# An H3 convolution with a gated linear unit, forward and backward, on one core: the GLU's forward pass moved four tiles ahead into the FFT stage, transposing loads for the weight gradients, one SBUF arena

## The chip, the core and the metric

The kernel runs on one core of a Trainium2 chip. The metric is the device time of one execution in microseconds. Names of engines: PE (TensorE, matrix products and transposes), DVE (VectorE), ACT (ScalarE), POOL (GpSimd), SP (SyncE, used here only to issue DMAs). SBUF is the on-chip memory of 128 partitions, PSUM the accumulators that PE writes and that DVE or ACT must copy out ("evacuate"); DRAM is off the core and reached by DMA alone.

## The reference, cut to what matters

Inputs are bf16; S = 2048 tokens, D = 512 channels, F = 1376 hidden units. The kernel returns the output and the gradients of nine inputs for a given `grad_out`.

```python
xn = layernorm(A_q)                                   # [S, D], no affine part
ks = sum_t shift(A_k, by 3-t tokens) * shift_k[:, t]  # 4 taps per channel
kv = ks * A_v
y  = irfft(rfft(pad(kv, 2S)) * rfft(pad(ssm_k, 2S)))[:S] + kv * ssm_D   # per channel
s  = xn * y
h  = sigmoid(xn @ w_gate) * (xn @ w_up)               # [S, F]
z  = h @ w_down                                       # [S, D]
out = A_q + s * silu(z)
# and the vjp of out with respect to q, k, v, shift_k, ssm_k, ssm_D, w_gate, w_up, w_down
```

The outputs are `out_0` (out), `out_1` to `out_3` (dq, dk, dv), `out_4` to `out_6` (the small gradients of shift_k, ssm_k, ssm_D), `out_7`, `out_8` (of w_gate, w_up, [512, 1376]) and `out_9` (of w_down, [1376, 512]).

## The kernel before, in words

**Tiles.** The 2048 tokens are 16 tiles of 128: partition p and tile j hold token 16p + j. The 512 channels are four groups `cg` of 128. F is padded to 1408, eleven blocks `fb` of 128. The FFT of length 4096 is done as matrix products with cosine and sine tables: `Cf` (forward, made at the start from integer tables, line 61), `Ci` (its transpose, for the inverse), and two small matrices `BD` and `R`.

**Stage 1, FFT forward and convolution.** For each channel group: the filter's block is transposed to token order (`KC`); step 1 multiplies by `Cf` (`ps_q`, L144, copied to `QgK` or `QgV`); PE transposes flip the axes (`ps_fl`, L156); step 3 multiplies by `BD` (`ps_xre`, `ps_xim`, copied to `KFg` or `Xc`). The shift convolution of k runs on DVE (`ks_term`, L352). DVE multiplies the two spectra (`cm_t`, L202 and 203, then `Y`, L208), PE goes back with `R` (`ps_b`, L179, 180) and `Ci` (`ps_y`, L193, 194). y goes to DRAM (`y_d`). Spectra go to DRAM too (`KF_d`, `KVF_d`), since the backward pass reads them. The order of these pieces is a list written by hand; transposes of the three GLU weights (L290, L295) are woven between them.

**Stage 2, the GLU, forward and backward, tile by tile.** LayerNorm (L438 to 447), `xnT` (L450), then `psG`, `psU` (L469, L473: the two projections), `sigT` (L476), `hT` (L477, h with F on the partitions), `psZ` (L507), the elementwise chain of the gate, `dz` and its transpose, `psD` (L562: dz by w_down), `dh` (L565), `dg` and `du` (L566, 567), `psX` (L579: back to dxn), the LayerNorm's gradient (`dxn` L583 to `goj` L594). For the weight gradients h, dg and du are also wanted with tokens on the partitions: `to_token_major` makes 33 PE transposes a tile (`ps_tmA`, `ps_tmB`, L489 and L493), copies them out (`stS_h`, `stS_dg`, `stS_du`) and stores them (`hS_d`, `dgS_d`, `duS_d`).

**Stages 3 and 4 together.** Two generators, interleaved one step to two: the FFT of the output's gradient and the inverse transforms for dkv and d ssm_k (same names, `B1g`, `B2g`; then `dksg`, the shift's gradient `dk_term` L755, the diagonal products), and the weight gradients: `psW` (L792) accumulates over the 16 token tiles from `L` (loads L786 of the token-major copies, 512 KB each) and `rhsA` (loads L780 of dz and of xn). The gradients of w_gate and w_up come out transposed there, with F on the partitions; 88 PE transposes (`ps_wT`, L803) and two copies (`w_ot`, `dwt`) turn them round.

PSUM is copied out by a fixed pattern of engines per call site (ACT alone, DVE alone, or two to one). SBUF is split in pools opened and closed by stage, so stage 2 starts when the pools of stage 1 are given back, and stage 3 after those of stage 2. The framework's scheduler puts each engine's instructions into one order; an engine works its own list in order.

Of the kernel before, what the change touches and what calls it, by code (L numbers as in the profile page):

```python
# [16 lines left out]
P = 128  # L17
# [12 lines left out]
JQ = 512 // GW  # L30
JC = 1
TC = JC * P
FPG = 512 // TC
# [8 lines left out]
def gen_fft_consts(nc, pre, fpool, tpool, pspool, ident):  # L42
    negpi = pre["negpi"]
    nc.vector.memset(negpi[:], -math.pi)
    sc = 2 * math.pi / 8192
    out = {}
    a = tpool.tile([P, 16], i32, name="cg_a")
    nc.gpsimd.iota(a[:], pattern=[[1, 16]], base=0, channel_multiplier=16)
    b = tpool.tile([P, 128], i32, name="cg_b")
    nc.gpsimd.iota(b[:], pattern=[[2, 128]], base=1, channel_multiplier=0)  # L50
    m = tpool.tile([P, 16, 128], i32, name="cg_m")
    nc.vector.tensor_tensor(m[:], a[:, :, None].to_broadcast([P, 16, 128]),
                            b[:, None, :].to_broadcast([P, 16, 128]), ALU.mult)
    mc = tpool.tile([P, 2, 16, 128], i32, name="cg_mc")
    nc.vector.tensor_single_scalar(mc[:, 0], m[:], 6144, ALU.add)
    nc.vector.tensor_single_scalar(mc[:, 0], mc[:, 0], 8191, ALU.bitwise_and)
    nc.vector.tensor_single_scalar(mc[:, 1], m[:], 8191, ALU.bitwise_and)
    mf = tpool.tile([P, 2, 16, 128], f32, name="cg_mf")
    nc.vector.tensor_copy(mf[:], mc[:])
    Cf = fpool.tile([P, 2, 16, 128], bf16, name="Cf")  # L60
    nc.scalar.activation(Cf[:], mf[:], ACT.Sin, bias=negpi[:], scale=sc)
    out["Cf"] = Cf
    Ci = fpool.tile([P, 2, 16, 128], bf16, name="Ci")
    out["Ci"] = Ci
    pi_ = tpool.tile([P, 1], i32, name="cg_pi")
    nc.gpsimd.iota(pi_[:], pattern=[[0, 1]], base=0, channel_multiplier=1)
    pa = tpool.tile([P, 1], i32, name="cg_pa")
    nc.vector.tensor_single_scalar(pa[:], pi_[:], 3, ALU.arith_shift_right)
    pe = tpool.tile([P, 1], i32, name="cg_pe")
    nc.vector.tensor_single_scalar(pe[:], pi_[:], 7, ALU.bitwise_and)  # L70
    paf = tpool.tile([P, 1], f32, name="cg_paf")
    nc.vector.tensor_copy(paf[:], pa[:])
    pef = tpool.tile([P, 1], f32, name="cg_pef")
    nc.vector.tensor_copy(pef[:], pe[:])
    cb = tpool.tile([P, 16, 8], f32, name="cg_cb")
    nc.gpsimd.iota(cb[:], pattern=[[1, 16], [0, 8]], base=0, channel_multiplier=0,
                   allow_small_or_imprecise_dtypes=True)
    ce = tpool.tile([P, 16, 8], f32, name="cg_ce")
    nc.gpsimd.iota(ce[:], pattern=[[0, 16], [1, 8]], base=0, channel_multiplier=0,
                   allow_small_or_imprecise_dtypes=True)  # L80
    ab = tpool.tile([P, 16, 8], i32, name="cg_ab")
    nc.vector.tensor_scalar(ab[:], cb[:], paf[:, 0:1], None, ALU.mult)
    mask = tpool.tile([P, 16, 8], f32, name="cg_mask")
    nc.vector.tensor_scalar(mask[:], ce[:], pef[:, 0:1], None, ALU.is_equal)
    ang = tpool.tile([P, 3, 16, 8], i32, name="cg_ang")
    nc.vector.tensor_single_scalar(ang[:, 0], ab[:], 12, ALU.add)
    nc.vector.tensor_single_scalar(ang[:, 1], ab[:], 8, ALU.add)
    nc.vector.tensor_copy(ang[:, 2], ab[:])
    nc.vector.tensor_single_scalar(ang[:], ang[:], 15, ALU.bitwise_and)
    angf = tpool.tile([P, 3, 16, 8], f32, name="cg_angf")  # L90
    nc.vector.tensor_copy(angf[:], ang[:])
    tri = tpool.tile([P, 3, 16, 8], f32, name="cg_tri")
    nc.scalar.activation(tri[:], angf[:], ACT.Sin, bias=negpi[:], scale=2 * math.pi / 16)
    nc.vector.tensor_tensor(tri[:], tri[:], mask[:, None, :, :].to_broadcast([P, 3, 16, 8]), ALU.mult)
    BD = pre["BD"]
    nc.vector.tensor_copy(BD[:], tri[:].rearrange("p t b e -> p t (b e)"))
    out["BD"] = BD
    R = pre["R"]
    trif = tri[:].rearrange("p t b e -> p t (b e)")
    nc.vector.tensor_scalar(R[:, 0, 0, :], trif[:, 0, :], SCALE_INV, None, ALU.mult)  # L100
    nc.vector.tensor_scalar(R[:, 0, 1, :], trif[:, 1, :], SCALE_INV, None, ALU.mult)
    nc.vector.tensor_scalar(R[:, 1, 0, :], trif[:, 2, :], SCALE_INV, None, ALU.mult)
    nc.vector.tensor_scalar(R[:, 1, 1, :], trif[:, 0, :], SCALE_INV, None, ALU.mult)
    out["R"] = R
    return out


class Evac:

    def __init__(self, nc, pattern="av"):  # L110
        self.nc = nc
        self.pattern = pattern
        self.i = 0

    def __call__(self, dst, src, eng=None):
        if eng is None:
            eng = self.pattern[self.i % len(self.pattern)]
            self.i += 1
        if eng == "a":
            self.nc.scalar.copy(dst, src)  # L120
        elif eng == "v":
            self.nc.vector.tensor_copy(dst, src)  # L122
        else:
            self.nc.gpsimd.tensor_copy(dst, src)


def gen_ci(nc, consts, pspool, ident):
    Cf, Ci = consts["Cf"], consts["Ci"]
    for c in range(2):
        for jh in range(2):  # L130
            pt = pspool.tile([P, 8, 128], bf16, name="ps_ci", tag="tr")
            for jj in range(8):
                nc.tensor.transpose(pt[:, jj, :], Cf[:, c, 8 * jh + jj, :], ident[:])
            nc.scalar.copy(Ci[:, c, 8 * jh:8 * jh + 8, :], pt[:])


def fft_fwd_step1_group(nc, consts, xsrc, cg, Qg, psum_pool, ev):
    Cf = consts["Cf"]
    for c in range(2):
        for jb in range(NJ // JQ):  # L140
            ps = psum_pool.tile([P, JQ, GW], f32, name="ps_q", tag="mm")
            for jj in range(JQ):
                j = jb * JQ + jj
                nc.tensor.matmul(ps[:, jj, :], Cf[:, c, j, :], xsrc(j), start=True, stop=True)  # L144
            src = ps[:].rearrange("p j (g e) -> p j g e", e=8)
            dst = Qg[:, c, :, jb * JQ:(jb + 1) * JQ, :].rearrange("p g j e -> p j g e")
            ev(dst, src)


def fft_flip_group(nc, Qg, Qf, ident, psum_pool, ev):  # L150
    for c in range(2):
        for gb in range(GG // 8):
            pt = psum_pool.tile([P, 8, 128], bf16, name="ps_fl", tag="tr")
            for gi in range(8):
                g = gb * 8 + gi
                nc.tensor.transpose(pt[:, gi, :], Qg[:, c, g].rearrange("p j e -> p (j e)"), ident[:])  # L156
            ev(Qf[:, c, gb * 8:(gb + 1) * 8, :], pt[:])


def fft_fwd_step3_chunk(nc, consts, Qf, qq, psum_pool):  # L160
    BD = consts["BD"]
    qre = Qf[:, 0, 4 * qq:4 * qq + 4, :].rearrange("p g k -> p (g k)")
    qim = Qf[:, 1, 4 * qq:4 * qq + 4, :].rearrange("p g k -> p (g k)")
    ps_re = psum_pool.tile([P, 512], f32, name="ps_xre", tag="mm")
    nc.tensor.matmul(ps_re[:], BD[:, 0, :], qre, start=True, stop=False)
    nc.tensor.matmul(ps_re[:], BD[:, 1, :], qim, start=False, stop=True)
    ps_im = psum_pool.tile([P, 512], f32, name="ps_xim", tag="mm")
    nc.tensor.matmul(ps_im[:], BD[:, 2, :], qre, start=True, stop=False)
    nc.tensor.matmul(ps_im[:], BD[:, 0, :], qim, start=False, stop=True)
    return ps_re, ps_im  # L170


def fft_inv_step3_chunk(nc, consts, Yc, qq, Bg, psum_pool, ev):
    R = consts["R"]
    for half in range(2):
        ps = psum_pool.tile([P, 2, 256], f32, name="ps_b", tag="mm")
        for gi in range(2):
            gg = 2 * half + gi
            nc.tensor.matmul(ps[:, gi, :], Yc[:, 0, gg, :], R[:, 0].rearrange("p a b -> p (a b)"), start=True, stop=False)  # L179
            nc.tensor.matmul(ps[:, gi, :], Yc[:, 1, gg, :], R[:, 1].rearrange("p a b -> p (a b)"), start=False, stop=True)  # L180
# [36 lines left out]
def kernel_impl(ctx, tc, A_q, A_k, A_v, A_shift_k, A_ssm_k, A_ssm_D, B_x, B_w_gate, B_w_up, B_w_down,  # L217
# [80 lines left out]
    if 1 in phases:  # L298
        with tc.tile_pool(name="p1fft", bufs=2) as fp_, \
# [63 lines left out]
            def B(cg):  # L363
# [522 lines left out]
```

## Time and profile before

| what | value |
|---|---|
| median of three runs | 794.98 us (789.26, 794.98, 797.74) |
| span of the profiled execution | 786.8 us, 14908 instructions |
| PE busy | 640.2 us (81%) |
| DVE busy | 509.3 us (65%) |
| ACT busy | 342.1 us (43%) |
| POOL busy | 179.2 us (23%) |
| granted PE clock, mean | 0.937 |
| DMA | 108.22 MB, mean 138 GB/s |

The profiled execution has no separate time outside the profile: its span, from the first to the last instruction, is 786.8 us, 2.5 us below the lowest of the three runs and 8.2 us below their median. Rows of the timeline give start, duration, engine, line, operation and tile, and in square brackets the idle time ahead of the instruction and what ended it. In the groups, the two figures after the bar are the group's busy time in us and the mean of one in ns; after the next bar stand the engine's idle time ahead and its releaser. "PEclk" is the clock that the PE was granted, as a share of full speed.

### The profile page before, as it was taken

How to read it: one execution, taken by the hardware profiler on the slowest of the kernel's cores; microseconds unless marked ns; L12 is line 12 of the kernel's file. 1: busy time of each engine (PE TensorE's matmuls, PEld its weight loads, DVE VectorE, ACT ScalarE, POOL GpSimd, SP SyncE). 2: the span in 40 equal slices, each digit the busy share in tenths (PEclk: the TensorE clock that was granted, in tenths of full speed). 3: DMA queues.
4: the chain of work that ended last, by engine and by line, in shares of the span. 5: the costliest groups of instructions: out<-in, count | busy, mean ns of one | idle time of the engine just before them, and what ended most of it. 6: DMA issues, size and time to landing. Idle time of an engine off the chain costs nothing. (4 is left out here: it accounts for less than half of the span.)

```text
span 786.8 us, 14908 instructions
## 1 busy us (share of the span) xinstructions
PE 640.2 (81%) x5936; PEld 432.5 (55%) x5936; DVE 509.3 (65%) x1154; ACT 342.1 (43%) x642; POOL 179.2 (23%) x263
## 2 busy tenths in 40 slices
PE   3446878783899999999999998079969789979885
PEld 2435556552777776677777775045635355555542
DVE  5677533473688888888888787018469059459571
ACT  5546889873344343334444333025515124524310
POOL 1102212132222222322233212400103021421311
PEclk9978899997799999999999999579989899999998
DMA  6754422143233333333333223995355754763546
GB/s 159 245 156 131 130 59 95 41 135 106 74 107 120 110 110 110 116 123 128 143 117 135 104 83 123 301 256 165 83 177 145 230 139 134 194 211 101 121 159 125
DMA packets 75488, 108.22 MB, mean 138 GB/s; under 512 B 25789, under 2 KB 60473, under 8 KB 74906
## 3 DMA queue, kind: packets, MB, share of 16 engines
q0 software_dynamic: 17232, 57.68, 23.9%
q1 hardware_dynamic: 47034, 41.16, 17.9%
q10 hardware_dynamic: 11152, 8.42, 3.7%
q8 instruction: 46, 0.75, 0.4%
q14 instruction: 24, 0.20, 0.1%
HBM read 55.87 MB, written 50.89 MB: 136 GB/s over the span
## 5 line engine op out<-in xcount | busy, mean ns | idle before, releaser
L122 DVE CAST w_ot<-psW 128x512 bf16<-128x512 f32 x27 | 18.6, 687 | 80.7 <-PE psW L792 80.7
L473 PE MATMUL psU<-xnT,wu 128*128 128x128 bf16 x704 | 54.8, 221 | 0.0
L144 PEld LDWEIGHTS <-Cf 128*128 128x128 bf16 x384 | 30.4, 112 | 39.9 <-issue 17.1
L469 PE MATMUL psG<-xnT,wg 128*128 128x128 bf16 x704 | 51.1, 223 | 0.6 <-DVE ln_ve L441 0.6
L120 ACT COPY stS_dg<-ps_tmA 128x1024 bf16<-128x1024 bf16 x16 | 16.2, 1012 | 73.8 <-PE ps_tmA L489 73.8
L120 ACT COPY dwt<-ps_wT 128x512 bf16<-128x512 bf16 x22 | 12.9, 588 | 81.2 <-PE ps_wT L803 62.7
L562 PE MATMUL psD<-dzT,wdT 128*128 128x128 bf16 x704 | 47.7, 221 | 0.2 <-DVE hT L477 0.2
L565 ACT CAST dh<-psD 128x512 bf16<-128x512 f32 (+1 forms) x48 | 26.4, 549 | 49.3 <-PE psD L562 44.7
L507 PE MATMUL psZ<-wd,hT 128*128 128x512 bf16 x176 | 41.9, 381 | 3.8 <-DVE hT L477 3.8
L469 PEld LDWEIGHTS <-wg 128*128 128x128 bf16 x704 | 43.5, 100 | 1.0 <-issue 0.8
L473 PEld LDWEIGHTS <-wu 128*128 128x128 bf16 x704 | 43.9, 99 | 0.0
L806 POOL DMA_DIRECT2D out_dram<-dwt x22 | 16.6, 756 | 118.8 <-ACT dwt L120 118.8
L562 PEld LDWEIGHTS <-wdT 128*128 128x128 bf16 x704 | 42.1, 99 | 0.3 <-issue 0.3
L579 PE MATMUL psX<-wgT,dgT 128*128 128x512 bf16 x176 | 40.6, 379 | 0.0
L579 PE MATMUL psX<-wuT,duT 128*128 128x512 bf16 x176 | 40.6, 379 | 0.0
L792 PE MATMUL psW<-rhsA,L_7574 128*128 128x512 bf16 x64 | 19.1, 420 | 24.0 <-DMA L_7574<-hS_d 24.0
L531 POOL DMA_DIRECT2D out_dram<-xj x16 | 9.1, 569 | 124.2 <-DVE xj L517 124.2
L122 DVE COPY QfV<-ps_fl 128x1024 bf16<-128x1024 bf16 x16 | 10.5, 687 | 33.5 <-PE ps_fl L156 33.1
L477 DVE TENSOR_TENSOR hT<-psU,sigT 128x512 bf16<-128x512 f32 (+1 forms) x48 | 30.7, 639 | 1.7 <-ACT sigT L476 1.7
L144 PE MATMUL ps_q<-KC,Cf 128*128 128x128 bf16 x128 | 13.0, 265 | 22.9 <-DVE KFg L122 10.6
L476 ACT ACTIVATE sigT<-psG 128x512 bf16<-128x512 f32 (+1 forms) x48 | 26.9, 561 | 6.5 <-PE psG L469 6.0
L579 PEld LDWEIGHTS <-duT 128*128 128x128 bf16 x176 | 17.2, 98 | 20.8
(782 smaller groups left out, 1774.6 us busy)
## 6 DMA issues: line engine op xcount, KB each, us to landing
hS_d<-stS_h POOLq DMA_DIRECT2D x16, 352.0 KB, 2.8
dgS_d<-stS_dg POOLq DMA_DIRECT2D x16, 352.0 KB, 2.5
duS_d<-stS_du POOLq DMA_DIRECT2D x16, 352.0 KB, 2.8
KF_d<-KFg POOLq DMA_DIRECT2D x4, 1024.0 KB, 4.7
KVF_d<-Xc POOLq DMA_DIRECT2D x16, 256.0 KB, 2.5
KFc<-KF_d SPq DMA_DIRECT2D x16, 256.0 KB, 3.2
KVFc<-KVF_d SPq DMA_DIRECT2D x16, 256.0 KB, 3.0
out_dram<-dwt POOLq DMA_DIRECT2D x20, 128.0 KB, 4.0
```

The source lines that it names most:

```text
L120: self.nc.scalar.copy(dst, src)
L122: self.nc.vector.tensor_copy(dst, src)
L144: nc.tensor.matmul(ps[:, jj, :], Cf[:, c, j, :], xsrc(j), start=True, stop=True)
L469: nc.tensor.matmul(psG[:, i, :], wg[:, db, fb * 128:(fb + 1) * 128], xnT[:, db].rearrange("p j t -> p (j t)"), start=(db == 0), stop=(db = ...
L473: nc.tensor.matmul(psU[:, i, :], wu[:, db, fb * 128:(fb + 1) * 128], xnT[:, db].rearrange("p j t -> p (j t)"), start=(db == 0), stop=(db = ...
L476: nc.scalar.activation(sigT[:, f0:f0 + nb_, :], psG[:, 0:nb_, :], ACT.Sigmoid)
L477: nc.vector.tensor_tensor(hT[:, f0:f0 + nb_, :], psU[:, 0:nb_, :], sigT[:, f0:f0 + nb_, :], ALU.mult)
L507: nc.tensor.matmul(psZ[:], hT[:, fb, jj * P:(jj + 1) * P], wd[:, fb, :], start=(fb == 0), stop=(fb == NFB - 1))
L562: nc.tensor.matmul(psD[:, i, :], wdT[:, db, fb * 128:(fb + 1) * 128], dzT[:, db].rearrange("p j t -> p (j t)"), start=(db == 0), stop=(db ...
L565: nc.scalar.copy(dh[:, 0:nb_, :], psD[:, 0:nb_, :])
L579: nc.tensor.matmul(psX[:], srcT[:, fb, jj * P:(jj + 1) * P], wT[:, fb, :], start=(i == 0 and fb == 0), stop=(i == 1 and fb == NFB - 1))
L792: nc.tensor.matmul(acc[:], L[:, j, b * 128:(b + 1) * 128], rhsA[:, j, :], start=(j == 0), stop=(j == NJ - 1))
```

## The change

The kernel is written anew around the same arithmetic.

- **SBUF** is one tile, `slab`, of 206 KB a partition; `Arena` hands out pieces of it by first fit and takes them back, `Ring` holds one or several buffers of a shape. PSUM has three kinds of buffers for the whole kernel: 4 `mm`, 2 `acc`, 2 `tr`.
- **`Bal`** counts estimated ACT and DVE time as the program is written out and gives each evacuation to the engine with the smaller sum. **`run_streams`** interleaves generators in proportion to their progress.
- **Stage A** runs three streams: `gluA` (xnT, psG, psU, sigma and h of the first four tiles), `frontA` (filter transposes, shift convolution, step 1) and `backA` (flips, `Ci`, step 3, spectra's product, inverse). y, xn, later dz stay in SBUF (`y2A`, `xnA`, `dzA`); both spectra of a quarter go to one DRAM tensor `KK_d`.
- **Stage B** works tile i's backward part with tile i+1's z and tile i+4's projections. No token-major copies are made: `hT`, `dgT`, `duT` go to DRAM as they are. `wdT` comes by a transposing DMA from DRAM.
- **Stage C** runs `frontC`, `backC` and `dW`. `L` is filled by 36 transposing DMAs (`dma_start_transpose`, L743) of up to 512 KB; there is a ring of two. `dW` multiplies xn (as the stationary operand) by dg and du, so that the gradients of w_gate and w_up come out as they are stored. dk and dv are stored per channel group. `inv3` orders `R` so that one evacuation of 512 replaces two of 256.

The core of the diff:

```diff
+LAG = 4
+def run_streams(streams, until=None):
+    live = [[g, 0.0, float(tot)] for g, tot in streams]
+    ...
+        order = sorted(live, key=lambda s: s[1] / s[2])
+    ...
+    run_streams([(gluA(), LAG * 11776), (frontA(), 4 * 10240), (backA(), 4 * 36864 + 4096)])
-    def to_token_major(srcT, nm, dst_d, j):
-        ...
-            nc.tensor.transpose(ptA[:, fb, :], srcT[:, fb, :], ident[:])
-        ...
+        nc.gpsimd.dma_start(hT_d[i * P:(i + 1) * P, :], hT.rearrange("p a t -> p (a t)"))
+        ...
+    nc.sync.dma_start(wd[:, 0:NFB - 1, :], B_w_down[0:128 * (NFB - 1), :].rearrange("(fb p) d -> p fb d", p=P))
+    nc.sync.dma_start_transpose(wdT[:, :, 0:F], B_w_down)
+        ...
+    def ld_L(n):
+        ...
+        for q in range(4):
+            nc.sync.dma_start_transpose(L[:, 0:nb, 4 * q:4 * q + 4, :].rearrange("p f j t -> p f (j t)"),
+                                        srcs[s][q * 512:(q + 1) * 512, f0 * 128:(f0 + nb) * 128])
+        ...
+                for db in range(4):
+                    acc = ps_acc([4, 128], name="psW")
+                    for j in range(NJ):
+                        nc.tensor.matmul(acc[:, 0:nb, :], xnA[:, j, db * 128:(db + 1) * 128], L[:, 0:nb, j, :],
+                                         start=(j == 0), stop=(j == NJ - 1))
+    ...
+    run_streams([(frontC(), 4 * 4096), (backC(), 4 * 40960 + 4096), (dW(), 35 * 8192)])
```

In the order of the changed program every SBUF operand is called `slab`, so there the line tells which it is. Three places follow.

ACT in the first stage, between two channel groups: before, evacuations of y, of the woven weight transposes (`ps_wt`) and of step 1.

```order
L120 CAST KFg<-ps_xre 128x512 x2
L120 CAST KFg<-ps_xim 128x512
L120 CAST y2s<-ps_y 128x512 x2
L120 COPY wdT<-ps_wt 128x4x128
L120 COPY wgT<-ps_wt_926 128x512
L120 COPY wuT<-ps_wt_932 128x512
L120 COPY KC<-ps_kt 128x1024 x2
L120 CAST QgK<-ps_q 128x4x16x8 x4
```

ACT at such a place in the changed program; L310 is the sigmoid of the GLU's gate, L288 the LayerNorm of a tile, L121 the evacuation chosen by `Bal`.

```order
L121 CAST slab<-ps_x 128x512 x2
L121 CAST slab<-ps_b 128x2x16x16 x4
L121 CAST slab<-ps_y 128x4x128
L310 ACTIVATE slab<-psG 128x512
L121 CAST slab<-ps_q 128x4x16x8 x4
L310 ACTIVATE slab<-psG 128x512
L121 CAST slab<-ps_q 128x4x16x8 x4
L288 ACTIVATE slab<-slab 128x512
```

The copies of weight transposes have left this place, and sigmoids and a LayerNorm of the GLU stand between the evacuations of step 1.

DVE in the second stage, from the first step of one tile's LayerNorm gradient on: before, the copies `stS` of the token-major transposes and the next tile's statistics (`ln_st`) lie between the steps.

```order
L583 SCALAR_TENSOR_TENSOR dxn,s_3657<-psX,dxa 128x512
L122 COPY stS_dg<-ps_tmB 128x384
L586 SCALAR_TENSOR_TENSOR junk,s_3660<-dxn,xn 128x512
L588 SCALAR_TENSOR_TENSOR cb<-s_3657,rstd_all 128x1
L590 SCALAR_TENSOR_TENSOR cc<-s_3660,rstd_all 128x1
L122 COPY stS_du<-ps_tmA 128x1024
L438 BN_STATS ln_st<-xj 128x6
L593 SCALAR_TENSOR_TENSOR u_3666<-xn,cc,u_3666 128x512
L122 COPY stS_h<-ps_tmA 128x1024
L594 TENSOR_TENSOR goj<-u_3666,goj 128x512
L122 COPY stS_h<-ps_tmB 128x384
```

The same engine and place in the changed program: L664 to L669 are the LayerNorm gradient, L599 to L618 the next tile's gate and output chain, L643 and L644 dg and du.

```order
L664 SCALAR_TENSOR_TENSOR slab<-psX,slab 128x512
L665 SCALAR_TENSOR_TENSOR slab<-slab 128x512
L666 SCALAR_TENSOR_TENSOR slab<-slab 128x2
L668 SCALAR_TENSOR_TENSOR slab<-slab 128x512
L669 TENSOR_TENSOR slab<-slab 128x512
L599 TENSOR_TENSOR slab<-psZ,slab 128x512
L602 TENSOR_TENSOR slab<-slab 128x512
L612 TENSOR_TENSOR slab<-slab 128x512
L603 TENSOR_TENSOR slab<-slab 128x512
L613 TENSOR_TENSOR slab<-slab 128x512
L604 TENSOR_TENSOR slab<-slab 128x512
```

The copies and the statistics are gone from between the steps.

SP in the last stage, before: the loads of `L`, of dz (`rhsA`), of dy and of the spectra stand in one queue.

```order
L780 DMA rhsA<-dz_d 128x2048 x4
L786 DMA L_7574<-hS_d 128x4x512
L648 DMA dyA<-dy_d 128x4096
L786 DMA L_7574<-hS_d 128x4x512 x3
L682 DMA KFc<-KF_d 128x2x512
L684 DMA KVFc<-KVF_d 128x2x512
L786 DMA L_7971<-hS_d 128x4x512 x4
```

SP in the changed program, from the last loads of stage B's grad_out (L573) on; L743 are the transposing loads, L792 the loads of the spectra, L842 a piece of the shift's gradient.

```order
L573 DMA slab<-in_grad_out_dram 128x512
L743 DMA_TRANSPOSE slab<-hT_d 128x4x512 x3
L792 DMA slab<-KK_d 128x2x1024 x2
L743 DMA_TRANSPOSE slab<-hT_d 128x4x512
L743 DMA_TRANSPOSE slab<-hT_d 128x3x512 x4
L743 DMA_TRANSPOSE slab<-dgT_d 128x4x512 x4
L792 DMA slab<-KK_d 128x2x1024
L743 DMA_TRANSPOSE slab<-dgT_d 128x4x512
L792 DMA slab<-KK_d 128x2x1024
L743 DMA_TRANSPOSE slab<-dgT_d 128x4x512
L792 DMA slab<-KK_d 128x2x1024
```

The loads of dz and dy are gone; those of `L` transpose, and the spectra's loads still stand behind them in the same queue.

1448 lines of the change are left out of this document (739 added, 709 removed).

## The prediction, made before the changed kernel ran

> **What bounds the kernel now.** I began with the page's slices and then cut the span where the stages change: step 1 of the FFT starts at 17 us, the last `ps_y` ends near 189, the weight gradients start near 511. In the stretches the columns are length, then busy time and count of PE, PEld, DVE, ACT, POOL, then PEclk, DMA share and GB/s.
>
> ```profile
> PE   3446878783899999999999998079969789979885
> 0.00:17.00 17.00, 4.04 (x21) 2.17 (x22) 9.64 (x21) 10.35 (x9) 3.79 (x13) 1.00 0.70 159
> 17.00:94.00 77.00, 47.81 (x394) 35.13 (x394) 54.04 (x71) 46.34 (x83) 11.27 (x14) 0.87 0.55 162
> 94.00:189.00 95.00, 71.48 (x718) 50.69 (x715) 42.01 (x83) 76.50 (x154) 21.95 (x31) 0.98 0.27 87
> 189.00:228.00 39.00, 27.94 (x296) 22.00 (x297) 24.19 (x72) 10.52 (x16) 8.11 (x15) 0.78 0.25 79
> 228.00:488.00 260.00, 254.38 (x2991) 189.53 (x2989) 217.80 (x624) 105.35 (x174) 71.84 (x128) 1.00 0.34 119
> 488.00:511.00 23.00, 1.49 (x18) 0.96 (x16) 3.78 (x11) 2.19 (x3) 9.90 (x8) 0.60 0.98 286
> 511.00:757.00 246.00, 214.13 (x1420) 123.69 (x1418) 146.29 (x258) 87.93 (x199) 46.54 (x48) 0.94 0.59 163
> 757.00:787.00 30.00, 18.88 (x92) 8.33 (x92) 11.57 (x17) 2.93 (x5) 5.81 (x8) 0.82 0.60 136
> ```
>
> The reader should see three kinds of stretch. From 228 to 488 PE is full at full clock: fewer PE columns are less time. Before 189 nobody is full; that stretch is a relay of PE, evacuations and DVE. From 488 to 511 and around 197 PE stands still, on a stage's border:
>
> ```profile
> 196.70 0.61 PE L450 MATMUL ps_xnT<-ident,xn 128*128 128x128 bf16 x4 [10.97 <-ACT xn L447]
> 510.64 2.98 PE L792 MATMUL psW<-rhsA,L_7574 128*128 128x512 bf16 x7 [21.06 <-DMA L_7574<-hS_d]
> ```
>
> The second wait is for loads that may start only when stage 2's pools are free: DMA share 0.98 in that stretch.
>
> **The change, stage B first,** since its terms are the surest. The pace of PE comes from starts, not from durations, which overlap:
>
> ```profile
> 250.54 1.06 PE L469 MATMUL psG<-xnT,wg 128*128 128x128 bf16 x16
> 251.44 1.06 PE L473 MATMUL psU<-xnT,wu 128*128 128x128 bf16 x16
> 257.83 2.54 PE L579 MATMUL psX<-wgT,dgT 128*128 128x512 bf16 x11
> 260.21 2.54 PE L579 MATMUL psX<-wuT,duT 128*128 128x512 bf16 x11
> 245.37 0.69 DVE L583 SCALAR_TENSOR_TENSOR dxn<-psX,dxa 128x512 f32<-128x512 f32 x1 [0.55 <-PE psX L579]
> 262.78 0.69 DVE L583 SCALAR_TENSOR_TENSOR dxn<-psX,dxa 128x512 f32<-128x512 f32 x1 [0.55 <-PE psX L579]
> L489 PE MATMUL ps_tmA<-ident,hT 128*128 128x128 bf16 x128 | 9.9, 220 | 0.1
> L122 DVE COPY stS_du<-ps_tmA 128x1024 bf16<-128x1024 bf16 x16 | 11.1, 691 | 0.0
> ```
>
> Sixteen matmuls of 128 columns take 0.90 us, 0.056 each; eleven of 512 take 2.38, 0.216 each. A tile takes 17.4 us (from one `dxn` to the next). The 33 token-major transposes a tile go: 33 × 0.056 = 1.85, leaving 15.6. They lay on PE's path, and nothing takes their place there. DVE was busy 217.80 of 260 us there, 14.6 a tile, and loses its copies (0.69 each and more) and the LayerNorm, so it falls to about 12 and stays behind PE. Four tiles' forward (88 projections and 4 transposes, 92 × 0.056 = 5.1 each) moves to stage A. The last four tiles of B, which have no forward beside them, would be 10.5 by PE; DVE's 10 to 11 and the chain from psZ to dz show more there: 11.5. So 12 × 15.6 + 4 × 11.5 = 233. At B's start `wd` must be loaded into space that stage A's last `ps_y` still reads (`Ci`), and then psZ and the gate's chain of tile 0 run alone:
>
> ```profile
> wd<-in_B_w_down_dram ACTq DMA_DIRECT2D x1, 1280.0 KB, 7.1
> ```
>
> 7.1 us of load and about 4 of chain, less 2 of transposes of `wgT`, `wuT` under them: 9. **B is 242**; before it was 488 − 189 = 299, the LayerNorm wait included. If `wd` is hidden, B is 233; if its load lands as slowly as `wu` in the loaded first stretch (15.9, quoted below), 251.
>
> **Stage A** takes in 4 × 5.1 = 20 us of PE work, which has room: PE was busy 123 of 189. DVE is what I think it fills:
>
> ```profile
> L352 DVE TENSOR_TENSOR ks_term<-kh,skb 128x2048 bf16<-128x2048 bf16 x12 | 14.6, 1220 | 1.1 <-DMA kh<-in_A_k_dram 0.9
> 732.93 0.69 DVE cm_t_9658 L202
> 733.62 0.60 DVE cm_t_9659 L203
> 734.56 0.33 DVE Y_9657 L208
> 734.89 0.35 DVE Y_9657 L209
> L438 DVE BATCH_NORM_STATS2 ln_st<-xj 128x6 f32<-128x512 bf16 x16 | 11.1, 693 | 14.4 <-DMA xj<-in_A_q_dram 14.0
> L477 DVE TENSOR_TENSOR hT<-psU,sigT 128x512 bf16<-128x512 f32 x32 | 21.8, 683 | 1.7 <-ACT sigT L476 1.7
> L122 DVE CAST w_ot<-psW 128x512 bf16<-128x512 f32 x27 | 18.6, 687 | 80.7 <-PE psW L792 80.7
> 16.96 2.74 PE L144 MATMUL ps_q<-KC,Cf 128*128 128x128 bf16 x24 [6.19 <-ACT Cf L61]
> wu<-in_B_w_up_dram ACTq DMA_DIRECT2D x1, 1376.0 KB, 15.9
> L120 ACT CAST QgK<-ps_q 128x512 bf16<-128x512 f32 x32 | 16.6, 630 | 13.3 <-PE ps_q L144 10.2 <-POOL wu L279 3.2
> L120 ACT COPY QfK<-ps_fl 128x1024 bf16<-128x1024 bf16 x16 | 16.8, 1101 | 1.4 <-PE ps_fl L156 1.4
> 13.20 3.71 ACT L61 ACTIVATE Cf<-cg_mf,negpi 128x4096 bf16<-128x4096 f32 x1
> ```
>
> By the order, DVE's list in A holds 32 shift operations × 1.22 = 39; 16 spectral products × (0.69 + 0.60 + 0.33 + 0.35) = 31.5; the statistics of all 16 tiles, pulled in from B, 11 with some 6 of small operations; 12 `hT` × 0.68 = 8; 39 evacuations of 512 × 0.69 = 27; 18 of 1024 bf16 × 0.69 = 12.5; 13 of weight transposes, some 5; the tables 9.6. Sum 149, of which 10 lie ahead of step 1. ACT's list is 137 evacuations of 512 × 0.63 = 86, 23 of 1024 × 1.10 = 25, and 12 sigmoids, 16 LayerNorms and 9 copies at some 0.6 with `Cf`'s 3.7, 26: 137. PE's 252,900 columns × 0.056 / 128 are 111. Both are below. The table `Cf` now stands on ACT behind tile 0's first sigmoid, which waits for `wg`, a load like `wu`'s; so step 1 starts near 20 instead of 16.96. An in-order DVE that also waits for PE now and then is perhaps 90% busy: 139 / 0.9 = 154, and **A is 174** (155 with DVE never waiting and a quick start; 200 if it is busy for 77%, between the 54.04 of 77 in the second stretch and this). Before: 189. Queued behind a DVE instruction that waits for ACT's sigmoid are now spectral products, which `inv3` waits for; that is the price in the 10%.
>
> **Stage C.** PE's columns after: the weight gradients keep 270,336; FFT, inverse and diagonal products keep 200,704; the 88 turning transposes go. By the order, 45,056 of these columns follow the last weight gradient, in the tail of channel group 3; 425,984 × 0.216 / 512 = 180 us precede it. The tail runs alone, a chain of one group: flips and step 3, 5.5; four quarters of two spectral products, 4 × 3.94 = 15.7; last inverse, 5.5; product with v 1.2; a DMA across partitions, 7 to 9; three taps with two operations each, 7.3; the store, by a load of the same shape 9.3 at most, and the end, about 8.
>
> ```profile
> 749.67 6.68 DMA dksg<-dksg
> vg_8016<-in_A_v_dram POOLq DMA_DIRECT2D x1, 512.0 KB, 9.3
> ```
>
> That is 51. 180 + 51 = 231. The wait of 21 us at 488 goes only if the first `L` are there: their ring overlies `wg`, `wu` and the sigmas, which the last forward (tile 15, in turn 11) frees, so job 0 has four tiles' time. dz, xn and dy stay in SBUF. For stalls on later `L` I add 14: **C is 245**; before 299.
>
> The unknown is the **transposing load**; nothing in the trace of before transposes in a DMA. Plain loads of the same bytes give bounds, per 512 KB:
>
> ```profile
> L_9816<-duS_d SPq DMA_DIRECT2D x4, 512.0 KB, 5.7
> L_9405<-duS_d SPq DMA_DIRECT2D x4, 512.0 KB, 10.5
> L_7574<-hS_d SPq DMA_DIRECT2D x4, 512.0 KB, 21.0
> q0 software_dynamic: 17232, 57.68, 23.9%
> q1 hardware_dynamic: 47034, 41.16, 17.9%
> ```
>
> Four in flight landing within 10.5 are 2.6 us each, the lower end; 21.0 each, one by one, is the upper. Between them: a packet of q0 (57.68 MB / 17232 = 3347 B) took 0.239 × 786.8 × 16 / 17232 = 0.175 us of an engine, one of q1 (875 B) 0.048; a line through both is 3 ns a packet and 0.051 ns a byte, so if such a load moves in 16384 pieces of 32 B, a guess between these ends, it takes 16384 × 4.7 ns / 16 = 5 us. I take 5: 32 of the 36 loads fall into C, 160 us, under the 180 of PE. C is the larger of 245 and 32t + 51, t being the time of one; they meet at t = 6. These loads stand on SP ahead of the spectra's (`KK`), which the products wait for; four transposing loads at 5 us are 20, about the two quarters by which `KK` is fetched ahead, and the 14 holds what is over.
>
> The Trainium skill, "DMA: Bandwidth & Descriptors", section "Latency and other measured facts", has 261 GB/s for a transposing DMA; an estimate by it is 2.0 us for 512 KB, C then 231 to 245, and the sum at most 14 less.
>
> **The sum.** 174 + 242 + 245 = 661 of span, against 786.8. The median of the three runs lies 8.2 above the span of before; the same 8 gives 669.
>
> **Rivals.**
> 1. *Stage A does not do what it says*: the forward tiles do not fill gaps but stand in the way. The relay of one channel group keeps its pace, A stays 189 and the 20 us of forward add to it: 209, total 669 + 35 = 704. For it: before, neither PE nor ACT nor DVE was full, so latency, not work, set the pace; and every engine works in order. Against it: the third stretch had ACT at 76.5 of 95 with DVE at 42, which `Bal` evens out.
> 2. *The transposing loads bind C, mildly*: t = 8 gives 32 × 8 + 51 = 307, total 669 + 62 = 731. For it: turning rows into columns is nothing a row of before shows; the 4 loads of 10.5 were already slow beside other traffic (share 0.59). Against it: 0.41 of the DMA time is free there.
> 3. *Slower than before*: the same place, the SP queue, with t above 10. C reaches 371 at t = 10, total 795; at 14, 923; at 21.0, one after the other, 32 × 21 + 51 = 723, total 1147. For it: one load of 21.0 in the trace, though that one stood among 6.6 MB of loads (286 GB/s in 23 us). Against: that rate itself, 1.8 us for 512 KB.
>
> The Trainium skill, "VectorE: DVE Perf Modes", section "The three transpose paths", gives 1309 ns for 128×128 by DMA against 390 ns by TensorE; that speaks against the change. An estimate by it is 16 × 1.309 = 21 us for a load, if its blocks go one by one. The trace has TensorE at 0.056 us a transpose and no DMA transpose, so it can't tell whether blocks overlap.
>
> **How the numbers follow.** The forecast 0.60, rival 1 0.13, rival 2 0.14, rival 3 0.13. The forecast's own range: A 155 to 200, B 233 to 251, C 231 to 260 are 619 to 711, with the 8, 627 to 719. Low end: below 620 all three must be best at once, 0.04. High end: rival 2 reaches up to 795; 780 (t = 9.5) leaves out rival 3 and a little. So 620 to 780. About 1% is what a measurement of this kernel can tell from no change: within 787 to 803 only a t near 10 lands, 0.03; slower 0.12; faster 0.85.
>
> **What the profile after would show.** A right: the last `ps_y` near 174 with DVE over 80% busy. B right: `dxn` to `dxn` 15.6, then 11.5; no PE wait over 10 us at its start. C right: PE over 85% busy until some 50 us before the end, few waits on `L`; a transposing load landing, four together, within about 20. Wrong: `psW` waits on `L` at every job of 4, or `inv3` on `KK`; a `dxn` distance set by DVE or ACT; A's end near 200. The forecast fails most easily by t, since it alone can move the sum by more than 50 us.

## The result and the profile after

The changed kernel takes 755.36 us (751.03 to 760.67, four runs) against 792.12 for the one before on the same chip: a ratio of **0.954**, 95% interval 0.946 to 0.961. It is faster, by 37 us where 126 were forecast. The profiled execution is 753.9 us long. Two lines of its page, and its stretches cut where the stages change (columns as before):

```profile
PE 586.7 (78%) x5340; PEld 386.3 (51%) x5340; DVE 443.5 (59%) x904; ACT 371.6 (49%) x588; POOL 146.0 (19%) x224
PE   2277386788879999999999789599949944996650
0.00:20.00 20.00, 4.24 (x24) 2.38 (x24) 9.57 (x22) 7.34 (x10) 7.98 (x18) 1.00 0.52 178
20.00:100.00 80.00, 45.05 (x423) 35.27 (x424) 56.40 (x93) 39.94 (x59) 11.54 (x21) 0.85 0.40 127
100.00:211.00 111.00, 88.69 (x981) 66.35 (x979) 76.60 (x152) 83.21 (x143) 23.31 (x41) 0.94 0.34 110
211.00:451.00 240.00, 229.71 (x2428) 159.91 (x2428) 181.62 (x450) 93.06 (x162) 42.56 (x74) 0.97 0.38 117
451.00:694.00 243.00, 194.53 (x1298) 106.89 (x1296) 90.31 (x142) 118.99 (x176) 55.19 (x65) 0.91 0.77 155
694.00:754.00 60.00, 24.51 (x192) 15.51 (x192) 28.97 (x48) 29.09 (x40) 5.44 (x7) 0.76 0.30 54
```

Stage A is now 0 to 211, B to about 452, C to the end. The slices show holes in PE again (a 5, a 4 and two 4s side by side), now in the last stage. In order: `ps_y` of stage A, `psZ` and the LayerNorm gradient's first step of stage B (after the durations stand the starts of the first and the last), PE's costliest holes in C, the chain behind the largest, and last what ACT waited for in all and how long the transposing loads took to land (median, us):

```profile
L440 PE MATMUL ps_y<-slab x128: 218/220/312, 93.2 to 209.4; 128*128 128x128 bf16 x128
L593 PE MATMUL psZ<-slab x176: 379/379/631, 215.6 to 431.9; 128*128 128x512 bf16 x176
L664 DVE SCALAR_TENSOR_TENSOR slab<-psX,slab x16: 684/692/693, 236.7 to 451.3; 128x512 f32<-128x512 f32 x16
479.31 3.57 PE L755 MATMUL psW<-slab 128*128 128x512 bf16 x8 [9.64 <-ACT slab L121]
557.33 3.36 PE L772 MATMUL psW<-slab 128*128 128x512 bf16 x8 [9.88 <-ACT slab L121]
632.33 1.86 PE L772 MATMUL psW<-slab 128*128 128x512 bf16 x4 [21.01 <-ACT slab L121]
631.69 1.07 ACT L121 CAST slab<-psW 128x512 bf16<-128x512 f32 x2 [23.20 <-DMA out_dram<-slab]
613.31 1.74 POOL L778 DMA_DIRECT2D out_dram<-slab  x3
608.94 4.46 POOL L809 DMA_DIRECT2D slab<-in_A_k_dram  x1
602.04 45.50 SPq L743 DMA_TRANSPOSE slab<-duT_d  x8
ACT slab L121 <- DMA out_dram<-slab: 61.0, 4, 23.2
slab<-hT_d SPq DMA_TRANSPOSE x12, 8.0
slab<-dgT_d SPq DMA_TRANSPOSE x12, 6.6
slab<-duT_d SPq DMA_TRANSPOSE x12, 6.3
```

The chain reads backwards: PE waits at 632 for an evacuation; ACT could not make it, because the three buffers `ot` were still being stored; POOL issued those stores at 613, and they landed 18 us later. ACT waits 61.0 us in this way. PE waits for `L` itself nowhere in the profile. The row of eight transposing loads joins two bursts of four, issued from 602.0 to 630.2 and from 638.6 to 647.6.

All ratios are of undisturbed executions, and where rows of e9_best and e17_lag2 are shown, whose profiles are of executions 1.6 to 1.9% above the fastest of their kernels, these two are compared with each other alone.

### The profile page after: what moved, and what is told of

Its sections match the earlier page's. It is cut to its first block, busy times and chain, and to the rows that moved or that the text cites. A ratio compares the mean times of both kernels' runs of the same rounds, so it can differ in the third digit from the quotient of the medians.

```text
span 753.9 us, 13216 instructions
## 1 busy us (share of the span) xinstructions
PE 586.7 (78%) x5340; PEld 386.3 (51%) x5340; DVE 443.5 (59%) x904; ACT 371.6 (49%) x588; POOL 146.0 (19%) x224
## 3 DMA queue, kind: packets, MB, share of 16 engines
q10 hardware_dynamic: 528, 1.41, 0.5%
## 5 line engine op out<-in xcount | busy, mean ns | idle before, releaser
L772 PE MATMUL psW<-slab 128*128 128x512 bf16 (+1 forms) x384 | 86.2, 370 | 30.9 <-ACT slab L121 30.9
L427 PE MATMUL ps_b<-slab 128*128 128x256 bf16 x384 | 63.0, 298 | 34.7 <-DVE slab L414 33.8
L658 PE MATMUL psX<-slab 128*128 128x512 bf16 x352 | 82.5, 390 | 0.4 <-DVE slab L643 0.3
L121 ACT CAST slab<-ps_b 128x512 bf16<-128x512 f32 x96 | 52.4, 592 | 53.3 <-PE ps_b L427 51.7
L772 PEld LDWEIGHTS <-slab 128*128 128x128 bf16 x384 | 37.4, 99 | 64.9 <-issue 34.4
L427 PEld LDWEIGHTS <-slab 128*128 128x128 bf16 x384 | 33.9, 104 | 67.4 <-DVE slab L414 54.7
L121 ACT CAST slab<-ps_q 128x512 bf16<-128x512 f32 x82 | 47.2, 616 | 43.1 <-PE ps_q L385 30.8
L121 ACT CAST slab<-psW 128x512 bf16<-128x512 f32 (+1 forms) x35 | 20.0, 575 | 83.3 <-DMA out_dram<-slab 61.0
L658 PEld LDWEIGHTS <-slab 128*128 128x128 bf16 x352 | 34.2, 100 | 41.5 <-issue 2.9
L755 PE MATMUL psW<-slab 128*128 128x512 bf16 x176 | 44.0, 397 | 9.6 <-ACT slab L121 9.6
L308 PE MATMUL psG<-slab 128*128 128x128 bf16 x704 | 49.1, 224 | 0.6 <-DVE slab L318 0.4
L316 PE MATMUL psU<-slab 128*128 128x128 bf16 x704 | 48.8, 223 | 0.3
L639 PE MATMUL psD<-slab 128*128 128x128 bf16 x704 | 46.6, 220 | 1.2 <-ACT slab L121 1.2
L308 PEld LDWEIGHTS <-slab 128*128 128x128 bf16 x704 | 44.0, 101 | 3.2 <-issue 1.9
L121 ACT CAST slab<-ps_x 128x512 bf16<-128x512 f32 x80 | 44.0, 626 | 1.5 <-PE ps_x L405 1.2
L639 PEld LDWEIGHTS <-slab 128*128 128x128 bf16 x704 | 42.2, 98 | 4.8 <-issue 1.2
L316 PEld LDWEIGHTS <-slab 128*128 128x128 bf16 x704 | 43.2, 100 | 0.9 <-issue 0.6
L121 ACT COPY slab<-ps_fl 128x1024 bf16<-128x1024 bf16 x39 | 37.5, 1041 | 11.9 <-PE ps_fl L395 11.7
```

Source lines behind the costliest of these rows:

```text
L308: nc.tensor.matmul(psG[:, b, :], wg[:, db, (f0 + b) * 128:(f0 + b + 1) * 128], xnT[:, db, :], start=(db == 0), stop=(db == 3))
L316: nc.tensor.matmul(psU[:, b, :], wu[:, db, (f0 + b) * 128:(f0 + b + 1) * 128], xnT[:, db, :], start=(db == 0), stop=(db == 3))
L427: nc.tensor.matmul(ps[:, gi].rearrange("p j x -> p (j x)"), Y[:, c, gg * 128:(gg + 1) * 128], R[:, c].rearrange("p j e c -> p (j e c)"), s ...
L639: nc.tensor.matmul(psD[:, b, :], wdT[:, db, (f0 + b) * 128:(f0 + b + 1) * 128], dzT[:, db, :], start=(db == 0), stop=(db == 3))
L658: nc.tensor.matmul(psX[:], srcT[:, fb, :], wT[:, fb, :], start=(n == 0), stop=(n == 2 * NFB - 1))
L755: nc.tensor.matmul(acc[:], L[:, b, j, :], dzA[:, j, :], start=(j == 0), stop=(j == NJ - 1))
```

## Experiments

All ratios are to the kernel before, with their 95% intervals; 0.01 is 7.9 us. The changed kernel's own is 0.954.

### More output buffers, and what else lies on ACT

```diff
-    ot_r = Ring(ar, [512], n=3)
+    ot_r = Ring(ar, [512], n=10)
```

> The ring of output buffers of the weight gradients gets 10 buffers instead of 3 (room comes from letting dk of the shift's gradient use v's buffer, and 1 KB more of slab). Theory T1: the last stage is long because ACT, which makes every evacuation there, waits for these buffers (9.6, 9.9 and 21.0 us of PE wait behind it, and 9 us at the end), so 35 to 50 us go, ratio to the changed kernel about 0.95. Theory T2: the transposing loads bind the stage and the waits only move to L; then less than 12 us go.

0.913 (0.906 to 0.921): 32 us less, T1's side and short of its 35. PE's largest waits now are others:

```profile
568.85 1.89 PE L427 MATMUL ps_b<-slab 128*128 128x256 bf16 x8 [8.81 <-DVE slab L414]
619.67 1.44 PE L771 MATMUL psW<-slab 128*128 128x512 bf16 x3 [10.06 <-DMA slab<-duT_d]
POOL slab L804 <- DMA out_dram<-slab: 45.9, 3, 19.3
```

With the waits on the buffers gone, a transposing load shows in one of PE's waits, 10 us: T2 holds for a part of what is left. The last row is a wait that the edit itself brought, v's load behind the store of dk that now uses v's buffer.

```diff
+    bal.a = bal.v = 0.0
     ld_KK(0)
```

> The two sums of Bal are set to zero at the start of the last stage, so that its evacuations are divided between ACT and DVE. T1 with ACT's list as the cause: 10 to 30 us go, since a wait for an output buffer then holds back only half of the evacuations. If the list does not matter and only the stores or the loads do: within 6 us.

0.952 (0.944 to 0.960): no gain. In the changed kernel all 215 evacuations of stage C are on ACT, since `Bal`'s sums run from the program's start and DVE's is far ahead by then. The edit divides less than expected: 190 stay on ACT and 25 go to DVE, and both then wait for output buffers, ACT 56.3 us and DVE 21.6 us in all. An even division is not tested.

```diff
-                pk = ps_mm([4, 128], name="ps_dk")
+                pk = ps_mm([128, 4], name="ps_dk")
...
-                bal.evac(dKT[:, :, 4 * jq:4 * jq + 4].rearrange("p n j -> p j n"), pk[:], 512)
+                bal.evac(dKT[:, :, 4 * jq:4 * jq + 4], pk[:], 512)
```

> ps_dk is accumulated as before, with the four token columns interleaved in PSUM, so that its evacuation writes runs of 8 bytes instead of single elements 32 bytes apart. ACT's 16 evacuations should take 0.6 instead of 2.7 us each, 33 us less of ACT. If ACT's list bounds the stage, 15 to 30 us go; if these evacuations lie beside other work, under 6.

0.953 (0.945 to 0.961), no gain, though the work went as expected. The group of these evacuations in the changed kernel, and in this one:

```profile
L121 ACT CAST slab<-ps_dk 128x512 bf16<-128x512 f32 x16 | 36.1, 2677 | 0.0
```

```profile
L121 ACT CAST slab<-ps_dk 128x512 bf16<-128x512 f32 x16 | 9.4, 587 | 3.4 <-PE ps_dk L852 3.4
```

26.7 us of ACT's time bought nothing: ACT still waits 60.9 us for the same buffers.

### The start of stage A

```diff
+    ld_KT(0)
+    ld_kv(0)
     nc.scalar.dma_start(wg[:, :, 0:F], ...
     ...
     gen_fft_consts(nc, ar, negpi, Cf, BD, R)
     ...
-    ld_KT(0)
-    ld_kv(0)
```

> The first loads of k, v and the filter get space of their own and are issued ahead of the weights, not in the space of the tables' temporaries after those are free. If the late start is what makes the first stage long, PE's wait of 11.4 us at 40 goes and 10 to 16 us with it; if the relay's pace sets the stage whatever its start, under 5.

0.930 (0.926 to 0.935): 18 us less, more than expected. In the changed kernel `Arena` had put k's buffer where the tables' temporaries lay, so its load was issued only at 21.6, DVE stood at the first shift, a step of the tables for `BD` and `R` (L204) stood behind that on DVE, and ACT behind this step:

```profile
21.59 0.70 SPq L452 DMA_DIRECT2D slab<-in_A_k_dram  x1
37.48 1.23 DVE L466 TENSOR_TENSOR slab<-slab 128x2048 bf16<-128x2048 bf16 x1 [10.52 <-DMA slab<-in_A_k_dram]
39.27 1.07 ACT L121 CAST slab<-ps_q 128x512 bf16<-128x512 f32 x2 [11.33 <-DVE slab L204]
39.90 0.59 PE L385 MATMUL ps_q<-slab 128*128 128x128 bf16 x4 [11.36 <-ACT slab L121]
```

The last `ps_y` moved from 209.4 to 200.6 only; the rest came in stage B. The new layout also moves `wd`, and the first psZ starts at 159 rather than 216, before the last `ps_y`.

```profile
L456 PE MATMUL ps_y<-slab x128: 218/220/308, 80.6 to 200.6; 128*128 128x128 bf16 x128
L594 PE MATMUL psZ<-slab x172: 379/379/631, 159.3 to 420.0; 128*128 128x512 bf16 x172
```

```diff
-    acc_r = Ring(ar, [NJ, GW])
+    acc_r = Ring(ar, [NJ, GW], n=2)
```

> The shift convolution's accumulator gets two buffers instead of one (h's ring gives up one of six for it), so that the next group's shift need not wait for the store of the last (9.4 us of DVE, 9.9 us of PE behind it). If such waits make up the first stage: 6 to 10 us less. If the relay catches up later: under 3.

0.929 (0.921 to 0.937), some 19 us less, twice the wait taken away. This edit too moves every buffer behind it in the arena; which part of the gain is the accumulator's stays open.

### What makes the stores late

```diff
-            nc.sync.dma_start_transpose(L[:, 0:nb, 4 * q:4 * q + 4, :].rearrange("p f j t -> p f (j t)"),
-                                        srcs[s][q * 512:(q + 1) * 512, f0 * 128:(f0 + nb) * 128])
+            nc.sync.dma_start(L[:, 0:nb, 4 * q:4 * q + 4, :].rearrange("p f j t -> p f (j t)"),
+                              srcs[s][q * 512:q * 512 + nb * 128, (f0 + nb - 4) * 128:(f0 + nb) * 128].rearrange("(p f) x -> p f x", f=nb))
```

> The 36 transposing loads become plain loads of the same bytes in pieces of 1 KB, as the kernel before had them; the transposition of h, dg and du is left out. T3, the transposing loads keep the DMA engines so long that the output stores land late and ACT waits for their buffers: with plain loads the waits on these buffers fall below 15 us in all (61 in the changed kernel) and 25 to 45 us go. T4, the stores are late for another reason (their own queue, other loads): under 8 us go.

0.924 (0.919 to 0.929): 23 us less, below T3's 25 to 45, and the waits on the buffers are not below 15:

```profile
ACT slab L121 <- DMA out_dram<-slab: 45.3, 4, 13.4
```

The gain lies between the two theories, and the waits are nearer to T4: transposing is a part of what makes the stores late, and not the larger one. T4's own run leaves the three buffers and the transposing loads, and changes the queue:

```diff
-                    nc.gpsimd.dma_start(out_9[r0:r0 + kf, :], ot[0:kf, :])
+                    nc.scalar.dma_start(out_9[r0:r0 + kf, :], ot[0:kf, :])
...
-                    nc.gpsimd.dma_start(o[db * 128:(db + 1) * 128, ...
+                    nc.scalar.dma_start(o[db * 128:(db + 1) * 128, ...
```

> The changed kernel with three output buffers, the stores of the weight gradients issued from ACT instead of POOL. If these stores are late because they stand in POOL's queue behind loads and stores of the channel group: the waits on the buffers fall from 61 to under 20 us and 20 to 35 us go. If the DMA engines are what they wait for: waits of 40 and more stay and under 8 us go.

0.893 (0.887 to 0.900), **48 us less by two words**, more than the 20 to 35 expected, and the waits as expected:

```profile
ACT slab L121 <- DMA out_dram<-slab: 17.3, 4, 7.3
449.00:711.00 262.00, 213.98 (x1476) 120.82 (x1474) 117.73 (x185) 147.83 (x215) 39.69 (x34) 0.93 0.82 153
```

In POOL's queue the stores stood behind the group's loads of v, k and the shifted k and its stores, most of them of 512 KB. In the changed kernel the stores that end ACT's four waits land with what was issued right ahead of them: at 478 with the load of k, at 556 and 632 with the 95 KB piece of the shifted k (L809), at 695 with the store of dk. That small piece takes 11.2 to 22.4 us from issue to landing, and still 11.2 to 12.5 with plain loads (e6_plain). Another engine's queue is not quicker in itself: the fastest of these stores lands in 1.9 us from POOL and in 3.1 from ACT. The Trainium skill, "DMA: Bandwidth & Descriptors", section "Rules for kernel authors", says that spreading DMAs over issuing engines doesn't help bandwidth; the rate in C did rise, from 135 GB/s (the last two stretches of the table above, by length) to 153, as it must when the same bytes pass in less time. What a second queue gives here is an order.

### The edits together, and what is left

These kernels combine the edits above; what differs between them stands in the expectations.

> Three edits together: nine output buffers, the early loads of k, v and the filter, and two accumulators in the shift. If the waits are independent, the gains add: 32 and 18 us as measured apart, with 6 to 10 for the accumulator, 50 to 60 in all, 695 to 705 us (ratio 0.88). If the stages share a bound behind them, 35 to 45.

0.910 (0.903 to 0.916): the gains did not add; e1_ot10 alone has 0.913. POOL's wait for v's buffer (42.6 us in all) took the rest, as the next run shows, which differs in this alone, with dk in the space of the first inverse's result:

```diff
-            dk = vg
+            dk = ar.view(B1_r.blks[0][0], [NJ, GW], bf16)
```

> As the three edits together, but dk lies in the space of the first inverse's result instead of v's buffer. In the run with v's buffer POOL waited 42.6 us in all to load v behind the stores of dk, with the output stores queued behind it. If that wait was on the path: 8 to 20 us less than there, near 708. If the DMA engines' time bounds the last stage (their share was 0.95 to 1.03 from 460 to 600): within 5 us of 723.

**0.872** (0.866 to 0.877), some 691 us by the ratio (the median of all four runs is 697), 30 less than with v's buffer, more than either reading allowed: no version that computes everything is faster, and it is 65 us under the changed kernel by the ratios.

> As e9_best with the 36 transposing loads made plain loads of the same bytes; the transposition is left out. If the transposing loads bind the last stage once the output buffers do not: 15 to 30 us less than e9_best. If they were late only behind other waits: under 5.

0.858 (0.856 to 0.861): 10 us less than e9_best, under the 15 expected and over the 5. Once the stores wait no longer, transposing costs about this. Here stage C is what the forecast had for it: 245 us from 435 on, PE full until the tail:

```profile
435.00:624.00 189.00, 185.18 (x1279) 103.65 (x1278) 88.92 (x138) 119.09 (x176) 55.91 (x61) 1.00 0.65 187
624.00:680.00 56.00, 25.69 (x200) 16.38 (x198) 28.97 (x48) 28.98 (x39) 4.92 (x6) 0.77 0.47 69
```

```diff
+            if cg == 0:
                 nc.gpsimd.dma_start(vg, vC[:, :, c0:c1])
                 ...
+            if cg == 3:
                 nc.gpsimd.dma_start(o3C[:, :, c0:c1], dkv)
                 ...
```

> As e9_best, but in the last stage the loads of v, k and the shifted k are made for the first channel group alone and the stores of dk, dv and the filter's gradient for the last alone; the other groups' results are left out. If the transposing loads are slow because these transfers share the engines with them: their median time to landing falls from 6 to 8 us to under 4.5 and 10 to 25 us go against e9_best. If they are slow by themselves: landing stays above 5.5 and under 6 us go.

0.867 (0.862 to 0.871), within the intervals of e9_best, and the loads land in 5.1 us (median): neither under 4.5 nor over 5.5. That the group's transfers slow the transposing loads is not shown.

> As e9_best, with the weight gradients' stores issued from ACT and ps_dk accumulated as before (evacuated in runs of 8 bytes). If POOL's queue and ACT's long evacuations still hold the last stage up: 10 to 25 us less than e9_best's 697, 672 to 687. If the transposing loads bind it now: within 6 us of 697.

0.884 (0.877 to 0.891), no faster than e9_best and rather slower: with nine buffers the stores have nothing to gain from ACT. PE's one large wait is for a transposing load, the DMA share is 0.93, and a store in ACT's own list now waits for a transposing load to land, so that the evacuation behind it stands 16.5 us:

```profile
457.86 4.61 PE L755 MATMUL psW<-slab 128*128 128x512 bf16 x12 [7.51 <-DMA slab<-hT_d]
458.27 0.58 ACT L121 CAST slab<-ps_q 128x512 bf16<-128x512 f32 x1 [16.47 <-DMA slab<-hT_d]
432.00:640.00 208.00, 192.53 (x1279) 110.35 (x1278) 88.65 (x138) 100.34 (x177) 37.40 (x27) 0.97 0.93 186
```

In the tail the DMA across partitions (L842) is used 19.1 us after its issue, against 6.5 in e10_bestplain. Either may be what makes this run slower; neither is tested.

> As e13_all with the two sums of Bal set to zero at the start of the last stage. If ACT's list, with every evacuation of that stage, is the bound once the waits are gone: 8 to 20 us less than e13_all; if not: within 5 us.

0.899 (0.890 to 0.909), slower than e13_all if anything. Again 25 of the 215 evacuations go to DVE; taking these off ACT's list gains nothing, and more was not tried.

### What paces stage A

```diff
             else:
+                continue
-                term = term_r.next()
-                nc.vector.tensor_tensor(term, src, skl, ALU.mult)
-                nc.vector.tensor_tensor(acc, acc, term, ALU.add)
```

> As e13_all, but three of the four taps of the forward shift convolution are left out, 24 operations of 1.22 us on DVE. If DVE's work paces the first stage, it ends 20 to 29 us earlier; if the relay between PE, the evacuations and DVE does, under 8 us.

0.893 (0.884 to 0.902), no gain, and the end of stage A did not move. e13_all, then this run:

```profile
L456 PE MATMUL ps_y<-slab x128: 218/219/308, 80.5 to 195.6; 128*128 128x128 bf16 x128
```

```profile
L456 PE MATMUL ps_y<-slab x128: 217/219/308, 82.3 to 196.1; 128*128 128x128 bf16 x128
```

29 us of DVE's work are worth nothing there: DVE is not what paces the stage. Which link of the relay does, PE, the evacuations or a wait between them, is not shown. The other suspect is the forward:

```diff
-LAG = 4
+LAG = 2
```

> The forward pass runs two tiles ahead instead of four, so two tiles' forward less stands in the first stage (10 us of PE) and two more tiles of the second have it beside them (2 x 4 us). If the forward only fills gaps in the first stage: its end moves by less than 3 us and the whole is 5 to 8 us longer. If it stands in the way there: the first stage ends 10 to 14 us earlier and the whole is 2 to 6 us shorter.

0.934 (0.927 to 0.941), 15 us less, more than either side; the rings of h and sigma shrink with LAG and the arena's layout moves again.

> As e13_all with the forward pass two tiles ahead instead of four. In the changed kernel two tiles fewer ended the first stage 7.4 us earlier while a tile of the second without forward took 13.9 us against 15.1, so by the traces 4 to 8 us less than e13_all. If the first stage's other waits had only hidden the forward: 0 to 5 us more.

> As e9_best with the forward pass two tiles ahead instead of four. If the forward stands in the way in the first stage, which DVE does not pace: its last ps_y comes 6 to 10 us earlier than the 196 of the other kernels with these edits, and the whole is 3 to 8 us shorter, 689 to 694. If it fills gaps: the end moves by less than 3 us and the whole is 2 to 5 us longer.

0.875 (0.868 to 0.882) and 0.874 (0.865 to 0.882), against 0.884 and 0.872 with four tiles: no difference that these runs can tell. The stages say more than the sums. e9_best with four tiles, then e17_lag2 with two:

```profile
L456 PE MATMUL ps_y<-slab x128: 218/218/308, 80.6 to 196.3; 128*128 128x128 bf16 x128
L665 DVE SCALAR_TENSOR_TENSOR slab<-psX,slab x16: 684/692/692, 221.9 to 431.4; 128x512 f32<-128x512 f32 x16
```

```profile
L456 PE MATMUL ps_y<-slab x128: 218/218/308, 76.8 to 186.8; 128*128 128x128 bf16 x128
L665 DVE SCALAR_TENSOR_TENSOR slab<-psX,slab x16: 691/692/693, 210.0 to 425.7; 128x512 f32<-128x512 f32 x16
```

In these two profiles two tiles' forward, 10 us of PE, end stage A 9.5 us later and save 3.8 in B. It fills hardly any gaps.

## Why the prediction was wrong, by its steps

| | forecast | measured | off |
|---|---|---|---|
| stage A | 174 | 211 | +37 |
| stage B | 242 | 241 | −1 |
| stage C | 245 | 302 | +57 |
| span | 661 | 753.9 | +93 |

**Stage A failed at the step "DVE is what I think it fills".** The sum of DVE's list was about right (149 forecast, 143 busy), but taking 29 us from it changed nothing (e15_taps); DVE was busy 68% of the stage where over 80% was the sign of being right, PE was busy 138 of 211 and ACT 130. What came true is the step of the first rival, the forward that stands in the way and adds its time. It had a chance of 0.13. That its 209 meets the 211 measured is in part luck: 14 us of the 211 are the two terms below, which it did not have, and by e9_best and e17_lag2 a stage with these two mended and without any forward would end near 177 (an estimate: 196.3 less twice 9.5), not at the 189 that it took from the kernel before. The rival's premise, that no engine was full before 189, stood in the stretches that the prediction quotes; DVE's 149 us of 174 were then taken for a bound because the sum was large, with no row in which PE waited only for DVE's throughput. Two further terms were missing. Where the arena puts the buffers decides when loads may start: 11 us of PE at the start (e4_early), not foreseen although the overlaps of the later stages were. And the shift's one accumulator buffer waits for its store. The two edits moved the last `ps_y` by 14 us together (209.4 to 195.6 in e13_all), and two tiles of forward by 9.5 more.

**Stage B** came out, by terms that cancel. Twelve tiles took 15.1 us each, 181 (187 forecast). The four without forward took 13.7, 14.2, 13.9 and, the last, 7.1, 49 together (46 forecast): in the first three PE waits for dz, the end of the next tile's gate chain (L604). The start, first `dxn` less one tile, took 10.6 (9 forecast):

```profile
402.52 0.69 DVE L664 SCALAR_TENSOR_TENSOR slab<-psX,slab 128x512 f32<-128x512 f32 x1 [1.54 <-PE psX L658]
416.18 0.68 DVE L664 SCALAR_TENSOR_TENSOR slab<-psX,slab 128x512 f32<-128x512 f32 x1
421.44 0.61 PE L624 MATMUL ps_dzT<-slab 128*128 128x128 bf16 x4 [3.25 <-DVE slab L604]
430.36 0.69 DVE L664 SCALAR_TENSOR_TENSOR slab<-psX,slab 128x512 f32<-128x512 f32 x1 [3.85 <-PE psX L658]
444.24 0.69 DVE L664 SCALAR_TENSOR_TENSOR slab<-psX,slab 128x512 f32<-128x512 f32 x1 [3.19 <-PE psX L658]
451.32 0.69 DVE L664 SCALAR_TENSOR_TENSOR slab<-psX,slab 128x512 f32<-128x512 f32 x1 [2.42 <-PE psX L658]
```

**Stage C failed at "For stalls on later `L` I add 14".** No stall on `L` came, and PE's three holes, 40.5 us together, came from elsewhere: output stores behind large transfers in POOL's queue (e11_actst, 48 us), felt through three buffers (e1_ot10, 32 us; the two cover the same wait). The prediction looked at SP's queue, where the new loads stand, and never at POOL's, where the stores have always stood. PE's columns and the tail were nearly right: in e10_bestplain 189 us, of which PE is busy 185 (180 forecast), and 56 (51 forecast). That they too make 245 is luck, since next to none of the 14 for stalls is in it. In the changed kernel PE is busy 194.5 us in the stretch before the tail, at a granted clock of 0.91 where e10_bestplain has 1.00; whether the clock is a cause here or follows from the holes is not shown. In the kernel before, the same kind of wait was there but smaller:

```profile
ACT dwt L120 <- DMA out_dram<-dwt: 16.2, 3, 7.9
```

The tail took 64 where 51 were forecast: its first evacuation waited 9.1 us for an output buffer, and the DMA across partitions took 14 us, not 7 to 9, for a reason that is not shown:

```profile
695.72 0.45 ACT L121 CAST slab<-psW 128x352 bf16<-128x352 f32 x1 [9.11 <-DMA out_dram<-slab]
725.39 0.62 SPq L842 DMA_DIRECT2D slab<-slab  x1
739.61 1.23 DVE L873 TENSOR_TENSOR slab<-slab 128x2048 bf16<-128x2048 bf16 x1 [9.11 <-DMA slab<-slab]
```

**The transposing load** was the announced unknown, and its 5 us came near by luck. The forecast guessed 16384 pieces of 32 B; the trace has pieces of 256 B, 2048 for a load of 512 KB. By the DMA views of the changed kernel the pieces of one load took 2.6 us of all 16 engines between 490 and 503, and 7.1 us between 602 and 631, beside the group's own transfers. Of the whole, transposing is worth about 10 us (e9_best and e10_bestplain), and 23 where the stores are late as well (e6_plain). Rivals 2 and 3 did not happen. With the engines nearly to itself, the load of `wdT`, 1.41 MB, landed in 7.3 us.

```profile
GB/s 0 0 0 0 0 0 0 60 164 197 129 135 228 256 285 287 293 287 290 293 288 291 290 290 293 287 293 290 290 291 288 293 290 287 294 288 293 164 53 0
slab<-in_B_w_down_dram SPq DMA_TRANSPOSE x1, 7.3
```

That is 290 GB/s while it runs, near the 261 of the Trainium skill ("DMA: Bandwidth & Descriptors", "Latency and other measured facts"), and it settles the other point of the Trainium skill that the prediction quotes: with 43 blocks of 128×128 in 7.3 us, 0.17 us each, blocks do not go one by one at 1309 ns ("VectorE: DVE Perf Modes", "The three transpose paths").

**The offset** of 8 us from span to median was 1.5 here. With stage B's 1 us it is what helped the forecast.

## What to carry to other kernels

An evacuation into a small ring that is stored from is a link to a DMA queue: before moving stores or loads, list what stands ahead of each store in its own queue, and give small frequent stores a queue of their own or enough buffers. Issued from an engine that also evacuates, a store that has to wait holds that engine up (16.5 us in e13_all). When one arena replaces pools, a buffer's address decides which earlier work its load waits for; read the overlaps at the start of the program first. A sum of an engine's work is a bound only where some row shows another engine waiting for that engine's throughput; in stage A, where all engines were part idle, 10 us of work on PE added 9.5, and 29 us of work taken from DVE gave nothing.

## What was not expected of the hardware

Evacuating 512 f32 from PSUM into single bf16 elements 32 bytes apart took ACT 2677 ns, against 587 in runs of 8 bytes (e3_dkform); on DVE it was 2363 ns (e2_bal) against 691 (e16_bal). A transposing load with the DMA engines nearly to itself moves 290 GB/s; beside other traffic in stage C the engines were busy 0.93 of the time at 186 GB/s (e13_all), where plain loads needed 0.65 for 187 (e10_bestplain).
